# Hash attention and Fourier mixing on one core: masks and sums of the first head pairs on TensorE, a shorter float64 conversion, and another place for w2

## The chip, the cores and the metric

The kernel runs on one core of a Trainium2 chip. The metric is the time of one execution in microseconds (us) on the device; a median of several executions is quoted. One of the first three executions of the kernel before took 2249 us; the two others lie between 1431.8 and 1436.9 us (0.4%), so that one is left out of every comparison. Only fast runs are compared.

## The reference, cut to what matters

```python
# q, k, v: (4, 8, 768, 64) float32; proj: (64, 6)
q_bits = (q @ proj > 0)                        # 6 hash bits for each row, k alike
mask   = q_bucket[..., :, None] == k_bucket[..., None, :]
scores = where(mask, q @ k.T / 8, -1e9)
attn   = exp(scores - max);  attn = attn / (sum(attn) + 1e-9)
x      = (attn @ v), heads side by side        # (4, 768, 512)
mixed  = real(fft(fft(x, axis=1), axis=2))
u      = x + mixed
un     = (u - mean(u)) / sqrt(var(u) + 1e-6)
out    = u + maximum(un @ w_ch1, 0) @ w_ch2    # (512, 2048), (2048, 512): float64
```

The two weight matrices come as float64. The kernel reads them as pairs of 32-bit words and makes float32 of them: 16 chunks of 128 x 512 for w1, 16 for w2. That is the "conversion" of this text.

## The kernel before: the parts that matter

The attention works on 16 pairs of heads (four per batch), each in six steps of 128 keys. The mixing of batch b runs between the steps of the attention of batch b+1. During the four pairs of batch 0 (stage A from here on) there is no mixing yet, and w1 is converted beside them. During pair 4 and after it, the first mixing and the conversion of w2 run.

```python
def narrow(dst, src, name):                   # one chunk: nine DVE operations, one GpSimd add
    tag[0] ^= 1
    st = wt([P, 5 * WC], F32, "zF"[tag[0]], name, 1)   # staged in z's and in F's buffer by turns
    nc.gpsimd.dma_start(raw.bitcast(I64), src)
    ...
    nc.gpsimd.tensor_tensor(dst, val, rest, op=ALU.add)

def weigh(n, g, c, prep):                     # one step, one half of the queries
    ...                                       # two score matmuls (one per head) into PSUM
    nc.scalar.activation(pk[:, :, 0:HALF], ps[:, :, 0:HALF], AF.Exp, scale=SCALE)
    for h in range(2):                        # the mask: bucket equal, times exp
        nc.vector.scalar_tensor_tensor(
            pk[:, h, 0:HALF], qb[:, h, qs], kb[:, h, c : c + 1], pk[:, h, 0:HALF],
            op0=ALU.is_equal, op1=ALU.mult)
...                                           # in attention():
            nc.vector.tensor_tensor(accs[g], ..., new[g][:, :, 0:HALF], op=ALU.add)   # the sums
...                                           # in mix(): F is the mixing's own tile, and later
        hall = wt([P, NFC, HALF], F32, "F", f"h{b}", 1)   # the hidden layer takes its buffer
...
other = both(weights([(w2, moe_w_ch2)]), other)           # w2 beside the first mixing
```

(`z` and `F` are tiles of the mixing.) The small tiles in PSUM, the memory that matmuls write to (transposes, hash bits, means, closing sums, h), come from a pool that has two buffers while attention runs. Every engine's order of instructions is fixed when the kernel is compiled.

## Time and profile before

| what | kernel before | read from |
|---|---|---|
| median time | 1432.6 us | runs |
| stage A | 18 to 239 us | stretches |
| first matmul of h, the hidden layer | 306.9 us | timeline of PE |
| last chunk of w2 finished | 369.3 us | timeline of POOL |
| first transpose after h (un), batch 0 | 423.9 us | timeline of PE |

A line of the page gives the busy time of each engine over the whole span of 1430.6 us:

```profile
PE 1270.0 (89%) x4642; PEld 618.0 (43%) x4642; DVE 791.5 (55%) x1429; ACT 269.6 (19%) x433; POOL 142.9 (10%) x174
```

PE is at 89% over the span, so a change that takes nothing off PE can win at most the other 160 us. The shares alone mislead here: DVE's 55% is an average over a stage in which it is the bound and a long rest in which it isn't.

A measure is the length of a head pair. Each pair is closed by a few matmuls with output `sum` on PE, after its last step; the time from one such close to the next is one pair's length. For the kernel before, the timeline of PE gives 63.5, 60.3 and 33.1 us for the pairs 1, 2 and 3; the last of these leaves out a preparation (see the cautions below the table of the experiments). The last w1 chunk was finished at 201 us, in pair 3.

### The profile page before, as it was taken

The page shows a single profiled execution, that of the slowest core. Times are in us where ns is not written, and L with a number is a line of the kernel's source. Part 1 is how long each engine was busy: PE and PEld are TensorE (multiplying, and loading weights), DVE is VectorE, ACT ScalarE, POOL GpSimd, SP SyncE. Part 2 cuts the span into 40 slices and gives each one's busy share as a digit, 9 for nine tenths or more (in the row PEclk, how much of TensorE's full clock was granted, in tenths as well). Part 3 has the DMA queues.
Part 4 walks back from the last instruction along what each step waited for, and adds up shares of the span by engine and source line. Part 5 has one row for each costly group of instructions (what it writes and reads, how often), then busy time and mean ns, then how long its engine had stood idle before and what let it go on. Part 6 is the DMA issues. An engine that isn't in the chain of part 4 may idle for free.

```text
span 1430.6 us, 11986 instructions
## 1 busy us (share of the span) xinstructions
PE 1270.0 (89%) x4642; PEld 618.0 (43%) x4642; DVE 791.5 (55%) x1429; ACT 269.6 (19%) x433; POOL 142.9 (10%) x174
## 2 busy tenths in 40 slices
PE   6685677770799999989999999999999999899996
PEld 2221223440354444456544544374544444754552
DVE  6988989889743445485544463665434453511010
ACT  3122223200212121131212221222121211000000
POOL 1432220123100000000000000000000000001000
PEclk9787979995899999999999999999999999999999
DMA  6212121022101010010101010101010000000000
GB/s 162 75 47 78 40 67 48 30 80 94 37 0 41 15 34 8 7 41 8 27 8 41 8 34 14 42 0 34 0 41 15 1 8 8 8 0 12 11 8 17
DMA packets 82578, 44.65 MB, mean 31 GB/s; under 512 B 76496, under 2 KB 76624, under 8 KB 82384
## 3 DMA queue, kind: packets, MB, share of 16 engines
q1 hardware_dynamic: 75856, 20.72, 6.3%
q0 software_dynamic: 6656, 23.07, 5.1%
q8 instruction: 38, 0.62, 0.2%
q14 instruction: 28, 0.23, 0.1%
HBM read 37.49 MB, written 6.29 MB: 31 GB/s over the span
## 4 chain that ended last, share of the span: by engine, by line
PE 69%; DVE 8%; issue 2%; ACT 1%; POOL 1%; DMA 0%; ACTq 0%; DVEq 0%; POOLq 0%
PE o L909 23%; PE h L881 23%; PE sc L703 7%; PE oo L721 6%; PE cs L830 2%; PE B L856 2%; PE A L856 2%; DVE pk L711 1%; PE sum L738 1%; PE bits L664 1%; DVE acc L776 1%; DVE st L583 1%; PE un L897 1%; PE trk L647 1%; PE trq L647 1%
## 5 line engine op out<-in xcount | busy, mean ns | idle before, releaser
L881 PE MATMUL h<-x,w 128*128 128x384 f32 x1024 | 343.5, 492 | 52.8 <-ACT h L890 52.3
L909 PE MATMUL o<-w,h 128*128 128x512 f32 x768 | 343.5, 597 | 1.4 <-DVE h L888 1.4
L711 DVE SCALAR_TENSOR_TENSOR pk<-qb,kb,pk 128x384 f32<-128x384 bf16 x384 | 230.4, 638 | 176.8 <-ACT pk L709 176.8
L881 PEld LDWEIGHTS h<-x,w 128*128 128x128 f32 x1024 | 191.9, 191 | 203.0 <-ACT h L890 53.0
L709 ACT ACTIVATE pk<-sc 128x768 f32<-128x768 f32 x192 | 148.1, 810 | 392.8 <-PE sc L703 267.5
L909 PEld LDWEIGHTS o<-w,h 128*128 128x128 f32 x768 | 141.1, 190 | 179.5 <-issue 171.2
L721 PE MATMUL oo<-pk,vn 128*64 128x384 f32 (+1 forms) x768 | 185.5, 517 | 21.7 <-DVE pk L711 16.2
L703 PE MATMUL sc<-qt,kt 64*128 64x384 f32 x768 | 179.1, 532 | 9.8 <-ACT pk L709 8.9
L888 DVE TENSOR_SCALAR h<-h 128x384 f32<-128x384 f32 x64 | 35.6, 556 | 165.3 <-PE h L881 165.3
L776 DVE TENSOR_TENSOR acc<-acc,pk 128x768 f32<-128x768 f32 x128 | 120.6, 954 | 2.7
L703 PEld LDWEIGHTS sc<-qt,kt 64*128 64x128 f32 x768 | 73.3, 192 | 98.2 <-issue 51.1
L721 PEld LDWEIGHTS oo<-pk,vn 128*64 128x64 f32 x768 | 55.2, 138 | 127.4 <-issue 58.0
L601 POOL TENSOR_TENSOR w<-st 128x512 f32<-128x512 f32 x32 | 78.8, 2462 | 248.1 <-DVE st L598 248.1
L890 ACT ACTIVATE h<-h 128x384 f32<-128x384 f32 x64 | 31.4, 491 | 358.4 <-PE h L881 292.6
L915 DVE SCALAR_TENSOR_TENSOR u<-o,rs,u 128x512 f32<-128x512 f32 x24 | 18.0, 750 | 135.4 <-PE o L909 135.4
L905 POOL TENSOR_SCALAR rs<-mv 128x1 f32<-128x1 f32 x24 | 7.3, 304 | 557.4 <-DVE mv L903 557.2
L830 PE MATMUL cs<-ch,z 128*128 128x256 f32 x192 | 50.7, 414 | 9.0 <-DVE z L817 8.8
L800 POOL DMA_DIRECT2D out_dram<-u x32 | 19.6, 612 | 364.5 <-DVE u L915 257.0
L830 PEld LDWEIGHTS cs<-ch,z 128*128 128x128 f32 x192 | 37.2, 204 | 26.1 <-DVE z L817 11.8
L856 PE MATMUL A<-sq,F 128*128 128x193 f32 (+1 forms) x192 | 36.9, 329 | 1.2 <-DVE x L872 1.2
L856 PE MATMUL B<-sq,F 128*128 128x193 f32 (+1 forms) x192 | 36.6, 327 | 0.7 <-DVE F L837 0.5
L899 ACT COPY u<-un 128x512 f32<-128x512 f32 x24 | 14.0, 585 | 121.6 <-PE un L897 121.6
(81 smaller groups left out, 841.9 us busy)
## 6 DMA issues: line engine op xcount, KB each, us to landing
st<-in_moe_w_ch_dram POOLq DMA_DIRECT2D x32, 512.0 KB, 4.1
qn<-in_q_dram SPq DMA_DIRECT2D x32, 192.0 KB, 3.3
kn<-in_k_dram SPq DMA_DIRECT2D x32, 192.0 KB, 3.5
vn<-in_v_dram SPq DMA_DIRECT2D x32, 192.0 KB, 3.2
out_dram<-u POOLq DMA_DIRECT2D x16, 256.0 KB, 2.4
out_dram<-u POOLq DMA_DIRECT2D x16, 128.0 KB, 2.6
sq<-k_sq SPq DMA_DIRECT2D x1, 1155.0 KB, 6.0
ch<-k_ch SPq DMA_DIRECT2D x1, 512.0 KB, 3.6
```

Of the source, the lines that this page charges most:

```text
L601: nc.gpsimd.tensor_tensor(dst, val, rest, op=ALU.add)
L703: nc.tensor.matmul(ps[:, h, 0:HALF], kt[rows, c * P : (c + 1) * P], qt[rows, qs], start=True, stop=True,)
L709: nc.scalar.activation(pk[:, :, 0:HALF], ps[:, :, 0:HALF], AF.Exp, scale=SCALE)
L711: nc.vector.scalar_tensor_tensor(pk[:, h, 0:HALF], qb[:, h, qs], kb[:, h, c : c + 1], pk[:, h, 0:HALF], op0=ALU.is_equal, op1=ALU.mult,)
L721: nc.tensor.matmul(oo[h * D : (h + 1) * D, 0:w], nat["v", n][:, c, h, :], pk[:, h, 0:w], start=(c == 0), stop=(c == NT - 1),)
L776: nc.vector.tensor_tensor(accs[g], first[g][:, :, 0:HALF] if c == 1 else accs[g], new[g][:, :, 0:HALF], op=ALU.add,)
L830: nc.tensor.matmul(ps[:, pc:DM:2], z[:, cp, pc, par, t * P : (t + 1) * P], ch[:, cp, pc, :], start=(cp == 0), stop=(cp == 1),)
L856: nc.tensor.matmul(ps[:, cols], f, sq[:, t, k, cols], start=(t == 0), stop=(t == NT // 2 - 1),)
L881: nc.tensor.matmul(ps, w1[:, c, fc * P : (fc + 1) * P], x[:, c, g * HALF : (g + 1) * HALF], start=(c == 0), stop=(c == NDC - 1),)
L888: nc.vector.tensor_scalar(hr, ps, 0.0, None, op0=ALU.max)
L890: nc.scalar.activation(hr, ps, AF.Relu)
L909: nc.tensor.matmul(ps, hs[fc][:, j * P : (j + 1) * P], w2[:, fc, :], start=(fc == 0), stop=(fc == NFC - 1),)
```

## The change

The intent: DVE is full in stage A, so its mask multiplications and its sums go to TensorE for the pairs of batch 0 (masks up to pair 5); the conversion gets shorter on DVE, with its test of the exponent on ScalarE; w2 is staged in z's buffer alone and issued behind the first part of the mixing, so that no chunk of w2 lies in the buffer that the hidden layer waits for. The next pair is also prepared ahead (its transposes and hash bits made), between the steps of the current one. The matmul of the mask adds 0 to a score where all six bits agree and -2^33 or less where one differs, so that the exponential gives 0 there.

```diff
+            nc.gpsimd.tensor_scalar(qk[:, 0], qk[:, 0], BIG, None, op0=ALU.mult)   # +-BIG/2, +-1/2 bits
...
+        if kb is None:                        # mask as a matmul of bits, added to the scores in PSUM
+            for h, rows in enumerate(heads):
+                nc.tensor.matmul(ps[:, h, 0:HALF], qb[rows, 1, ks], qb[rows, 0, qs],
+                                 start=True, stop=False)
...
+            if sums is not None:              # batch 0: sums by four 32-column matmuls a step
+                for i in range(4):
+                    nc.tensor.matmul(sums[32 * i : 32 * i + 32, :], ones[:, 0:32],
+                                     pk[i // 2][:, i % 2, 0:HALF],
+                                     start=(c == 0), stop=(c == NT - 1))
...
+            if b == 0:
+                sums = pt([P, HALF], f"sums{n}")       # a small PSUM buffer, for the whole pair
+            else:
+                accs = [...]
...
+        nc.scalar.activation(mask, hi, AF.Abs)         # the test of the exponent, on ScalarE
+        nc.scalar.activation(mask, mask, AF.Abs, bias=mid[:, 0:1])
+        nc.scalar.activation(mi, mask, AF.Sign, bias=mid[:, 1:2])
...                                                    # then five DVE operations for nine
+            st = wt([P, 2, 3 * WC], F32, "z", f"st{wdr.shape[0]}", 1)     # two slots in z's buffer
...
+            ahead = prepare(n + 1) if n + 1 < NPAIR * B else iter(())
...
-            other = both(weights([(w2, moe_w_ch2)]), other)
+        other = after(NPAIR + NT, other, weights(w2, moe_w_ch2))
```

## The prediction

> **What bounds the kernel now.** I read the page's slices first, then the stretches, then the groups of the first stretch, then the waits of the gap. The slices show two different kernels in one span: for the first ten slices (358 us) TensorE (PE) is half to three quarters busy and its granted clock moves between 0.5 and 0.9, while VectorE (DVE) is near full; from slice 11 on PE is at 9 and the clock at full speed.
>
> ```profile
> PE   6685677770799999989999999999999999899996
> DVE  6988989889743445485544463665434453511010
> ACT  3122223200212121131212221222121211000000
> PEclk9787979995899999999999999999999999999999
> ```
>
> The stretches, cut where the trace has its stage borders (columns: length, busy us and instruction count of PE, weight load, DVE, ACT = ScalarE, POOL = GpSimd, then the clock):
>
> ```profile
> 18.00:239.00 221.00, 162.67 (x576) 54.50 (x577) 199.41 (x376) 54.84 (x84) 63.13 (x31) 0.84 0.24 61
> 239.00:307.00 68.00, 56.54 (x239) 34.90 (x240) 61.23 (x107) 12.85 (x18) 12.59 (x15) 0.92 0.11 35
> 307.00:365.00 58.00, 6.05 (x18) 2.98 (x18) 54.30 (x94) 0.15 (x1) 19.80 (x19) 0.59 0.30 102
> 365.00:409.00 44.00, 42.88 (x163) 22.03 (x164) 24.66 (x48) 11.09 (x20) 1.26 (x1) 0.96 0.08 18
> 409.00:1248.00 839.00, 825.62 (x3138) 410.94 (x3137) 425.94 (x756) 174.28 (x280) 34.12 (x72) 1.00 0.08 19
> ```
>
> From 18 to 239 us (stage A: head pairs 0 to 3 of batch 0, with w1 converted beside them) DVE is busy 199 of 221 us: it is the bound. From 239 to 307 (pair 4 and the mixing of batch 0) it still is. From 307 to 365 PE does nothing. After 365 PE never stops for long: it is the bound to the end. What DVE does in stage A, and what ended the gap:
>
> ```profile
> L711 DVE SCALAR_TENSOR_TENSOR pk<-qb,kb,pk 128x384 f32<-128x384 bf16 x96 | 62.2, 675 | 0.8 <-ACT pk L709 0.8
> L776 DVE TENSOR_TENSOR acc<-acc,pk 128x768 f32<-128x768 f32 x32 | 29.0, 946 | 0.0
> L592 DVE SCALAR_TENSOR_TENSOR st<-st 128x512 int32<-128x512 int32 x17 | 13.1, 771 | 0.0
> L583 DVE TENSOR_SCALAR st<-st 128x512 int32<-128x512 int32 x16 | 6.7, 417 | 0.0
> ```
>
> ```profile
> ACT h L890 <- POOL w L601: 65.7, 1, 65.7
> PEld h L881 <- ACT h L890: 53.0, 1, 53.0
> PE h L881 <- ACT h L890: 52.3, 1, 52.3
> ```
>
> The gap is a buffer wait: the tile that holds the hidden layer has the tag F, and the conversion of w2 stages every second chunk in that tag, so the first eviction of h waits for the last add (L601) of a w2 chunk in it. The timeline gives the pace there, one chunk per 5.53 us, DVE without a pause:
>
> ```profile
> 335.83 1.36 POOL L601 TENSOR_TENSOR w<-st 128x512 f32<-128x512 f32 x1 [3.31 <-DVE st L598]
> 337.49 0.55 POOL L572 DMA_DIRECT2D st<-in_moe_w_ch_dram  x1 [0.30 <-POOL w L601]
> 341.36 1.36 POOL L601 TENSOR_TENSOR w<-st 128x512 f32<-128x512 f32 x1 [3.31 <-DVE st L598]
> ```
>
> **What the Trainium skill says.** First, "ScalarE: Activation LUTs", What ACT_TABLE_LOAD costs: an ACTIVATE takes 186 ns and 0.833 ns an element, and about 93 ns more with a per-partition bias. The trace agrees: the exponential of 768 elements took 811 ns, the formula gives 826. Second, the same page, Table sets: cheap functions such as abs sit in every set, a change of set is a reload. The compiled change holds one table load, as before, so no reload is to be paid for Abs and Sign. Third, "TensorE: Matmul & The Clock Gate", Part 1: the array runs at half clock until it has been busy for one window of some 3.4 us and falls back after an idle one. The clock means 0.84 in stage A and 0.59 in the gap agree. Fourth, the same page, Part 3: matmuls in different 32-column strips run side by side. The four bit matmuls of 32 columns take 1.40 us at full clock here (833.90 to 835.30 us in the timeline), where four full ones would take 2.6 (the h rows: 24 instructions, 12 matmuls, in 7.94 us, so 0.66 us each).
>
> **The change, part by part.**
> DVE in stage A. Gone: 96 mask multiplications (62.2 us), all 40 acc additions (36 us), half the q and k evictions (5.4 us), the qb and kb copies (4.7 us). A chunk's conversion goes from nine DVE operations to five: 417 + 3 x 680 + 415 ns = 2.9 us where the rows of before add up to 5.0, so 16 chunks take 46 us where they took some 81. Added: 16 bit evictions of 0.55 us for 4 before (6.6 us). One reciprocal chain per pair for two saves about 8 us. What stays: 46 (conversion) + 9.9 (w1 minus its mean) + 11 (bits, with pair 5's) + 6.7 (reciprocals) + 4.8 (x) = 78 us, for 199. DVE is no bound any more.
>
> ScalarE in stage A. 48 exponentials x 0.81 = 39; evictions 20 x 0.415 + 10 x 0.478 = 13; squares 10; Abs, Abs with bias, Sign with bias per chunk 0.61 + 0.71 + 0.71 = 2.03 by the skill's formula, x 16 = 33; reciprocal evictions 4: 99 us for 55.
>
> PE per step (one block of 128 keys, 24 steps in stage A), full clock, from the rows of the steady part: scores 1.49, values 1.44; new masks about 0.4 (the four bf16 matmuls of 384 columns of qb took 0.43); sums of four 32-column matmuls 0.7 to 1.4, say 1.0; transposes and full-width bit matmuls (1.7 + 4 x 0.66) / 6 = 0.72; the two matmuls that spread the reciprocals 0.22; the means of w1 0.57. Sum 5.8 us. So PE alone would need 24 x 5.8 = 140 us.
>
> The conversion ring. Still two staging slots, and now each chunk goes through four engines in series. From the timeline: end of an add to the start of the next use of its slot 3.9 us (transfer and wake-up); three dependent ACT operations 2.1; four dependent DVE operations 2.6 (0.72 + 0.72 + 0.46 + 0.70); the add 1.35 with its wake-up. That is 10.1 us a slot, 5.05 us a chunk if nobody is in the way; among exponentials and evictions on the in-order ACT I take 12 us a slot, 6 a chunk. The compiled order puts the three ACT operations of all 16 w1 chunks ahead of the exponentials of step 10 or so of 24, thus the first steps go at the ring's pace.
>
> Sum to the end of stage A: first add at about 22 us as before (the start is the same load, transposes, bits); 7 more rounds x 12 = 84, the last chunk's Sign at about 101 us; 13.5 steps left at 5.8 plus some 0.7 for pair borders and single-buffered evictions (the sums hold one of the two small PSUM buffers throughout) = 88. Pair 4 starts at about 189 us where it started at 239: 50 us saved.
>
> Mixing and w2. The w2 slots lie in z's buffer, so the ring can start after the last cs matmul, which I put at pair 4's step 4: 189 + 28 = 217. Eight rounds of 12 us and a landing of 4 end it at about 317. In the compiled order the last w2 chunk stands on ACT beside h 12 and step 3 of pair 5; before reached that point at 409 us. So 92 us are saved there, not more, since PE alone would have been there 25 to 30 us sooner (h 12 x 2.65 + 2.5 steps x 4.1 + preparation, about 48 us after the first h at some 240). The gap of 52 us is gone, but part returns as ring waits between h matmuls.
>
> From there 1430.6 - 409 = 1022 us remain, the same work at the same full PE. Preparing the next pair ahead may take out the small waits at pair borders (0.7 us at pair 5, about 4 us at a batch border), 0 to 8 us in all. 317 + 1022 - 4 = 1335 us.
>
> **The rivals.** (1) The ring isn't felt: slots turn in 10 us, PE sets the pace. For it: the unloaded sum is 10.1, and DVE loses over half its load. Against it: both ACT and PE are in order, a wait for a transfer stands in front of an exponential. It would give 22 + 71 + 78 = 166 for stage A, the ring's end near 275, and 1295 us. (2) The chain gets longer than the ring: every exponential waits behind a conversion, every conversion behind an exponential that waits for PE at half clock; slots of 14 us, later steps of 7.5. For it: PE clock 0.84 in stage A already, one small PSUM buffer taken by the sums, 5.8 us then being an underestimate. It gives some 220 for pair 4 and 1385 us. (3) The expected gain is hidden because PE was the bound anyway. Against it: 52 us of plain PE idleness and 90% DVE in stage A; it would leave 1410 or so.
>
> **Range and chances.** The middle is 1335 us, between (1) and (2), nearer to (1) in mechanism but with the ring felt; 1300 to 1368 should hold it 8 times in 10. Even (2) is over 3% faster, so faster by over 2% has 0.97, within 2% 0.025, slower 0.005.
>
> **What would show it right or wrong.** DVE busy time in the stretch before pair 4 at about 80 us; ACT's idle time in its first 100 us ended by the w transfers; POOL adds of w1 every 6 us on average, the last near 105; pair 4's scores starting at 180 to 200 us; no PE gap above some 8 us after 20 us, but short PE waits on ACT during w2; the last w2 add at 310 to 325; 1015 to 1022 us from h 12 to the end. If adds come every 7 us or more, rival 2 holds; if PE is dense before the last w2 add, rival 1. The prediction fails most easily if the clock stays low in stage A or the adds on POOL stretch (they average 3.2 us before 270 us in the profile of before, 1.4 in the median).

## The result, and the profile after

The changed kernel takes 1350.48 us (median of 4, 1346.92 to 1354.56). The ratio to the kernel before is 0.942, with a 95% interval of 0.9375 to 0.9466. Ratios in this text are the mean time of one kernel's fast runs over that of the other's fast runs of the same rounds, so they are not quite the ratio of the quoted medians. A second set of five runs gave 0.9401 (x_after2 below).

The slices of the changed kernel, each 33.6 us long:

```profile
PE   5889999989999999999999999999999998999995
...
DVE  2655225886344626744444626754344635310110
...
PEclk9979999999999999999999999999999999999998
```

The hole in PE's row is gone, DVE's row has no 9 left, and from the fourth slice to the last but one PE is at 8 or 9 with the clock up. The stretches of the changed kernel, cut at its own stage borders (columns as in the prediction: length, then busy time and count of PE, weight load, DVE, ACT, POOL, then the clock):

```profile
18.00:199.00 181.00, 162.00 (x795) 60.80 (x798) 81.19 (x141) 86.69 (x142) 42.05 (x38) 0.94 0.28 75
118.00:199.00 81.00, 79.45 (x408) 29.98 (x408) 19.68 (x37) 29.43 (x48) 5.71 (x5) 1.00 0.13 30
232.00:328.00 96.00, 83.95 (x346) 47.06 (x344) 76.68 (x132) 47.53 (x74) 28.81 (x30) 0.96 0.31 99
```

Stage A is now 181 us (18 to 199), and DVE is busy for 81 of them where it was for 199 of 221. But look at the second line: in the second half of stage A PE is busy for 79.45 of 81 us at a clock of 1.00. DVE has 61 idle us there. The bound has moved to PE.

How long a pair takes with next to nothing left to convert can be read between the first exponentials of two pairs on ACT: such a stretch holds six steps and one preparation in both kernels. Pair 3 of the kernel before (columns as above):

```profile
200.32:240.38 40.06, 32.29 (x142) 12.23 (x140) 39.06 (x77) 13.09 (x21) 1.26 (x1) 0.94 0.13 30
```

And pair 2 of the changed kernel:

```profile
118.17:158.48 40.31, 39.46 (x204) 14.99 (x202) 7.91 (x15) 14.65 (x24) 2.91 (x3) 1.00 0.13 30
```

The pair takes 40.1 us before and 40.3 after. What has changed is the engine that is full: DVE before (39.06 us), PE after (39.46 us). So on its own a pair has not become faster; the change gains where the conversion used to hold DVE.

### The profile page after: what moved, and what is told of

It reads as the page before. It is cut to its first block, busy times and chain, and to the rows that moved or that the text cites. A ratio compares the mean times of both kernels' runs of the same rounds, so it can differ in the third digit from the quotient of the medians.

```text
span 1345.0 us, 12355 instructions
## 1 busy us (share of the span) xinstructions
PE 1275.1 (95%) x4902; PEld 631.4 (47%) x4902; DVE 610.6 (45%) x1081; ACT 337.1 (25%) x549; POOL 127.9 (10%) x192
## 4 chain that ended last, share of the span: by engine, by line
PE 78%; issue 7%; DVE 6%; POOL 3%; DMA 2%; ACT 2%; POOLq 0%; SPq 0%; ACTq 0%; DVEq 0%
PE o L987 25%; PE h L959 24%; PE sc L752 9%; PE oo L772 8%; PE cs L908 3%; DMA st<-in_moe_w_ch_dram 2%; POOL w L613 2%; DVE pk L761 2%; PE B L934 2%; PE A L934 2%; PE sum L808 1%; PE sums L827 1%; DVE acc L853 1%; PE un L975 1%; ACT pk L758 1%
## 5 line engine op out<-in xcount | busy, mean ns | idle before, releaser
L959 PE MATMUL h<-x,w 128*128 128x384 f32 x1024 | 344.4, 494 | 9.6 <-ACT qt L516 4.1
L761 DVE SCALAR_TENSOR_TENSOR pk<-qb,kb,pk 128x384 f32<-128x384 bf16 x240 | 137.7, 613 | 178.7 <-ACT pk L758 178.7
L752 PE MATMUL sc<-qt,kt 64*128 64x384 f32 x768 | 204.1, 515 | 2.5 <-ACT pk L758 2.5
L772 PE MATMUL oo<-pk,vn 128*64 128x384 f32 (+1 forms) x768 | 154.6, 505 | 0.8 <-DVE x L813 0.8
L752 PEld LDWEIGHTS sc<-qt,kt 64*128 64x128 f32 x768 | 83.3, 188 | 80.4 <-issue 59.0
L853 DVE TENSOR_TENSOR acc<-acc,pk 128x768 f32<-128x768 f32 x96 | 93.0, 972 | 15.0 <-ACT pk L758 13.2
L772 PEld LDWEIGHTS oo<-pk,vn 128*64 128x64 f32 x768 | 47.9, 137 | 94.5 <-issue 82.4
L613 POOL TENSOR_TENSOR w<-w,st 128x512 f32<-128x512 f32 x32 | 43.0, 1342 | 120.2 <-DVE st L610 109.9
L908 PE MATMUL cs<-ch,z 128*128 128x256 f32 x192 | 46.2, 389 | 4.3 <-DVE x L813 2.5
L592 ACT ACTIVATE st<-st 128x512 f32<-128x512 int32 x32 | 21.9, 684 | 60.4 <-DMA st<-in_moe_w_ch_dram 60.4
```

What stands on the lines that cost most here:

```text
L613: nc.gpsimd.tensor_tensor(dst, dst, rest, op=ALU.add)
L752: nc.tensor.matmul(ps[:, h, 0:HALF], kt[rows, ks], qt[rows, qs], start=kb is not None, stop=True,)
L761: nc.vector.scalar_tensor_tensor(pk[:, h, 0:HALF], qb[:, h, qs], kb[:, h, c : c + 1], pk[:, h, 0:HALF], op0=ALU.is_equal, op1=ALU.mult,)
L772: nc.tensor.matmul(oos[g][h * D : (h + 1) * D, 0:w], nat["v", n][:, c, h, :], pk[g][:, h, 0:w], start=(c == 0), stop=(c == NT - 1),)
L853: nc.vector.tensor_tensor(accs[g], first[g][:, :, 0:HALF] if c == 1 else accs[g], new[g][:, :, 0:HALF], op=ALU.add,)
L908: nc.tensor.matmul(ps[:, pc:DM:2], z[:, cp, pc, par, t * P : (t + 1) * P], ch[:, cp, pc, :], start=(cp == 0), stop=(cp == 1),)
```

## The experiments

Every experiment is an edit of the changed kernel. The first four ran on one chip, the next four on the same chip, the last four on another chip; the first and the last had their own runs of the kernel before, the second used those of the first and one more. All results are correct except that of x_noconv. The pair lengths are from the timeline of PE.

| run | us, median | ratio | 95% interval | pair 0 closes at | pairs 1, 2, 3 take | first un |
|---|---|---|---|---|---|---|
| before | 1432.6 | 1 | | 70.6 | 63.5, 60.3, 33.1 | 423.9 |
| changed kernel | 1350.5 | 0.942 | 0.9375 to 0.9466 | 77.9 | 45.6, 40.3, 38.3 | 336.9 |
| x_dvetest | 1353.5 | 0.9438 | 0.9423 to 0.9454 | 80.6 | 45.9, 40.3, 38.3 | 344.4 |
| x_raw3 | 1347.8 | 0.9401 | 0.9384 to 0.9417 | 82.8 | 41.8, 40.8, 38.3 | 334.6 |
| x_nolite | 1349.1 | 0.9422 | 0.9402 to 0.9443 | 63.8 | 46.7, 52.5, 40.6 | 335.6 |
| x_w1nine | 1348.9 | 0.9409 | 0.9392 to 0.9426 | 78.4 | 44.3, 40.5, 38.3 | 338.9 |
| x_noconv (wrong result) | 1313.9 | 0.9168 | 0.9146 to 0.9189 | 67.4 | 40.2, 40.5, 38.3 | 304.6 |
| x_sumsdve | 1323.7 | 0.9236 | 0.922 to 0.9251 | 62.1 | 44.8, 40.9, 28.0 | 313.1 |
| x_noahead | 1350.1 | 0.942 | 0.9405 to 0.9436 | 73.0 | 52.9, 34.7, 32.1 | 340.0 |
| x_onlyw2 | 1377.9 | 0.9616 | 0.96 to 0.9632 | 71.3 | 59.1, 58.5, 33.1 | 361.6 |
| x_hold | 1335.0 | 0.9304 | 0.9277 to 0.9331 | 63.7 | 43.3, 42.8, 32.7 | 320.7 |
| x_w2order | 1386.1 | 0.9657 | 0.9641 to 0.9673 | 78.7 | 49.9, 44.0, 38.3 | 375.2 |
| x_sums_raw3 | 1320.5 | 0.9202 | 0.9184 to 0.9219 | 66.9 | 43.3, 34.5, 28.0 | 306.4 |
| x_after2 (changed kernel) | 1350.0 | 0.9401 | 0.9383 to 0.942 | 76.5 | 46.8, 40.4, 38.3 | 337.3 |

Two cautions about the closes. With the sums on PE a close waits for the reciprocal on DVE and comes after the next pair's first scores: the last value matmuls of pair 0 start at 66.64 us in the changed kernel and its close at 77.91, where x_sumsdve has 60.79 and 62.13. And without preparing ahead (before, x_noahead, x_onlyw2) the closes of the pairs 0 to 2 come after the next pair's preparation, that of pair 3 before it, so the number for pair 3 lacks a preparation there. Where this matters, the text goes by the start of a pair's first exponential on ACT ("starts").

### x_dvetest: the exponent test back on DVE

```diff
-        nc.scalar.activation(mask, hi, AF.Abs)
-        nc.scalar.activation(mask, mask, AF.Abs, bias=mid[:, 0:1])
-        nc.scalar.activation(mi, mask, AF.Sign, bias=mid[:, 1:2])
+        nc.vector.tensor_scalar(mi, hi, 2**31 - 1, None, op0=ALU.bitwise_and)
+        nc.vector.tensor_scalar(mi, mi, float(897 << 20), -1.0, op0=ALU.is_ge, op1=ALU.mult)
```

> The changed kernel with one part undone: the exponent test of a conversion chunk goes back from three ScalarE operations (2.1 us in series) to two on VectorE (0.84 us). Theory ring: stage A and the w2 stage go at the pace of two staging slots, 13 us a round for w1 and 12 for w2 in the trace of the changed kernel; the round gets 1.2 us or more shorter and no exponential stands behind a transfer any more, so 7 rounds of w1 and 8 of w2 give 18 to 30 us: 1318 to 1330 us. Rival PE: PE and the small PSUM buffers set the pace, the ring is hidden: 1340 to 1352 us. Rival DVE: VectorE is still short in the w2 stage (77 of 96 us busy), 32 x 0.84 us more on it cost time: 1355 to 1370 us.

Measured: 1353.5 us, 3 us more by the medians, with intervals that overlap (0.9423 to 0.9454 against 0.9375 to 0.9466). What ScalarE took over in this part of the change is worth some 3 us, if anything.

### x_raw3: three staging slots

```diff
-            st = wt([P, 2, 3 * WC], F32, "z", ...)       # two slots of raw words and mask
+            st = wt([P, 3, 2 * WC], F32, "z", ...)       # three slots of raw words
-                    narrow(dst, src, s[:, 0 : 2 * WC].bitcast(I32), s[:, 2 * WC :])
+                    mask = wt([P, WC], F32, "u", ..., 2) # the mask in a buffer that is idle then
+                    narrow(dst, src, st[:, n % 3].bitcast(I32), mask)
```

> The changed kernel with three raw staging slots in the same bytes for two (the mask goes to a buffer that is idle then), nothing else changed. Theory ring: a round of 12 to 13 us now serves three chunks, 4.2 us a chunk where it was 6 to 6.5; stage A becomes PE's (pair 4's scores at about 180 us for 199.7) and the last w2 add comes by about 295 us for 327.5; 1300 to 1318 us. Rival PE: no change, 1340 to 1352 us. Rival ScalarE: the three operations on ScalarE themselves, not the slots, hold up the exponentials: between, 1325 to 1340 us.

This is the test of the prediction's pacing: if the ring of two slots sets the pace of the first steps, a third slot shortens them. Measured: the last w1 chunk was finished at 98.5 us where the changed kernel had 117.2, so the ring did turn faster, and the attention did not: pair 0 closes 5 us later, pair 1 takes 4 us less, the pairs 2 and 3 the same within 0.5 us, and the time is 1347.8 us, with an interval (0.9384 to 0.9417) that lies inside that of the changed kernel. What PE waits for has changed instead. The waits of PE in x_raw3 between 20 and 120 us (total us, times, longest):

```profile
PE sum L803 <- DVE rb L790: 5.8, 1, 5.8
PE bitsq L692 <- DVE qkb L693: 4.5, 1, 4.5
```

In the changed kernel the same two rows are 2.9 and 2.5. The conversions that come earlier stand on DVE, which works in the compiled order, among the operations of a reciprocal and in front of a bit eviction (at the end of pair 0, from the copy of `vs` to the last transpose of the reciprocal, six conversion operations stand between, 76.04 to 82.22 us, where the changed kernel has four, 72.51 to 77.27). So the number of slots isn't the bound.

### x_nolite: masks and sums back on DVE

```diff
-    LITE = 6
+    LITE = 0
-            if b == 0:
+            if b < 0:                                    # no sums on PE
-                elif b > 0:
+                elif b >= 0:                             # DVE sums in every batch
```

> The changed kernel with the first part undone: all masks and sums on VectorE again, the new conversion and the new place of w2 kept. Theory: VectorE's load before pair 4 goes from 80 us to about 185, so pair 4's scores start at 210 to 222 us for 199.7, and the w2 stage gets 31 us more VectorE work: 1368 to 1390 us. Rival: the new conversion alone already freed VectorE enough, the masks on TensorE only moved work: 1340 to 1355 us.

Measured: 1349.1 us, the same as with them on PE. DVE is full again (91.14 of 98 us between 20 and 118 us, 59.73 in the changed kernel), and in sum it costs nothing: pair 1 starts 9 us earlier than in the changed kernel (59.6 and 69.0 us), pair 3 at the same time (158.8 and 158.5). The first part of the change as a whole is worth zero beside the other parts; x_sumsdve below shows that this zero is a gain and a loss.

### x_w1nine: nine DVE operations for w1

The edit gives w1 the conversion of before, staged in the F buffer, which is idle in stage A; w2 keeps the short one.

```diff
+            if wsb is w1:
+                st = wt([P, 2, 5 * WC], F32, "F", "st_w1", 1)
...
+                    if wsb is w1:
+                        narrow9(dst, src, s)             # the nine operations of before
```

> The changed kernel with the nine VectorE operations of before for w1 alone (staged in two slots of the buffer that the mixing uses later), w2 as changed. Theory ring: with the masks gone VectorE has room for 16 x 2.1 us more, and ScalarE loses 33 us; the round stays near 12 us, pair 4's scores come at 190 to 203 us and the time is 1335 to 1352 us, so the shorter conversion is worth next to nothing in stage A. Rival: the saved VectorE operations are a real part of the gain there: 1360 to 1375 us.

Measured: 1348.9 us, no difference, though DVE is at 90.19 of 98 us between 20 and 118 us. With the masks and sums on PE, the shorter conversion of w1 is worth nothing either.

### x_noconv: hardly any conversion, with a wrong result on purpose

```diff
-        nc.scalar.activation(mask, hi, AF.Abs)
...                                                       # all ACT and DVE operations go
-        nc.gpsimd.tensor_tensor(dst, dst, rest, op=ALU.add)
+        nc.gpsimd.tensor_tensor(dst, hi.bitcast(F32), hi.bitcast(F32), op=ALU.add)
```

> Wrong result on purpose: the changed kernel with the conversion cut to its transfer and one GpSimd add a chunk; the eight ScalarE and VectorE operations are gone for both weights, so a round of the two slots falls to about 5.3 us (3.9 + 1.35). Three slots changed nothing (1347.8 us), so the slot count is not what holds stage A. Theory blocking: a conversion costs PE by standing in front of other work on in-order engines (in the run with three slots PE waited 5.8 and 4.5 us for VectorE, which had conversions ahead); without it pairs 0 and 1 take about the 40.4 us of pairs 2 and 3 instead of 49, and the w2 stage loses its 12 us of PE idleness: 1312 to 1326 us. Rival PE: the conversion is hidden behind PE's own work as it is: 1338 to 1350 us.

Measured: 1313.9 us (relative error 285.6). Both conversions together still cost 36 us in the changed kernel. More telling are the closes of the pairs 2 and 3 (timeline of PE in x_noconv):

```profile
148.16 1.56 PE L781 MATMUL sum<-rb,sel 128*128 128x384 f32 x4 [0.71 <-DVE rb L768]
...
186.48 1.56 PE L781 MATMUL sum<-rb,sel 128*128 128x384 f32 x4 [0.71 <-DVE rb L768]
```

Pair 3 takes the same 38.3 us, pair 2 takes 40.5 (40.3 in the changed kernel), and even pair 1 still takes 40.2 with no conversion at all. So a pair of the changed kernel takes 38 to 40 us because of PE's own work. By the closes, the conversion of w1 costs the changed kernel 77.9 - 67.4 = 10.5 us in pair 0 and 45.6 - 40.2 = 5.4 in pair 1, nothing in the pairs 2 and 3; that of w2 costs 77.7 - 66.9 = 10.8 us between the first h matmul and the first un (259.19 to 336.88 in the changed kernel, 237.65 to 304.56 here), and 57.0 - 51.2 = 5.8 before that, from the close of pair 3 to the first h matmul.

### x_sumsdve: masks on PE, sums on DVE

If PE is the bound, the next question is which of its new jobs is worth the place.

```diff
-            if b == 0:
+            if b < 0:                                    # no sums on PE
-                elif b > 0:
+                else:                                    # DVE sums in every batch
```

> Masks stay on TensorE, the denominators of batch 0 go back to VectorE additions. Theory PE: pairs 2 and 3 show PE dense (78.5 of 80 us) at 6.7 us a step, of which the sums take 0.79 and the spreading 0.25; so without them stage A is some 15 to 20 us shorter, VectorE (20 of 80 us busy there) has room for the 44 us: 1325 to 1336 us. Rival conversion: the first 100 us hang on the conversion, VectorE gets 22 us more in them and is in front of PE: 1345 to 1360 us.

Measured: 1323.7 us, 27 us faster than the changed kernel, with a correct result and DVE work put back. The closes of the pairs 2 and 3 in x_sumsdve (timeline of PE):

```profile
147.83 1.46 PE L808 MATMUL sum<-acc,ones 128*64 128x384 f32 x8
...
175.82 1.46 PE L808 MATMUL sum<-acc,ones 128*64 128x384 f32 x8
```

Pair 3 takes 28.0 us for 38.3 (163.83 to 202.16 in the changed kernel). With x_nolite as the third corner: masks and sums on DVE 1349.1, masks on PE and sums on DVE 1323.7, both on PE 1350.5 us. The masks on PE are worth 25 us; the sums on PE cost 27. In the traces x_sumsdve starts pair 1 7.0 us earlier than the changed kernel, pair 2 6.7, pair 3 12.7 and pair 4 22.5: the gain lies in the pairs 0, 2 and 3, and pair 1, beside the conversion (which ends at 130.6 us here), gains nothing.

Why so much, when the sums of a step took only 0.79 us? One step of the changed kernel, with half of the next pair's bit matmuls in it, from one start of the sums to the next (timeline of PE):

```profile
143.67 0.85 PE L827 MATMUL sums<-pk,ones 128*32 128x384 f32 x8
144.46 0.91 PE L692 MATMUL bitsq<-qt,pjw 128*128 128x384 f32 x2
145.30 0.34 PE L747 MATMUL sc<-qkb 64*128 64x384 bf16 x2
145.47 0.81 PE L752 MATMUL sc<-qt,kt 64*128 64x384 f32 x2
146.21 0.91 PE L692 MATMUL bitsq<-qt,pjw 128*128 128x384 f32 x2
147.05 0.59 PE L752 MATMUL sc<-qt,kt 64*128 64x384 f32 x1
...
148.70 1.51 PE L772 MATMUL oo<-pk,vn 128*64 128x385 f32 x8
150.14 0.53 PE L827 MATMUL sums<-pk,ones 128*32 128x384 f32 x4
```

And the same kind of step in x_sumsdve:

```profile
136.96 0.34 PE L747 MATMUL sc<-qkb 64*128 64x384 bf16 x2
137.13 0.81 PE L752 MATMUL sc<-qt,kt 64*128 64x384 f32 x4
137.78 0.33 PE L747 MATMUL sc<-qkb 64*128 64x384 bf16 x2
137.94 0.81 PE L752 MATMUL sc<-qt,kt 64*128 64x384 f32 x4
138.68 1.51 PE L772 MATMUL oo<-pk,vn 128*64 128x385 f32 x8
140.12 1.56 PE L692 MATMUL bitsk<-kt,pjw 128*128 128x384 f32 x4
141.61 0.34 PE L747 MATMUL sc<-qkb 64*128 64x384 bf16 x2
```

A float32 matmul is two records here, so "sc<-qt,kt x4" is the two heads of one block and "x2" one head alone. The two heads use 64 rows of the array each, and run side by side: 137.13 to 137.78, 0.65 us for both. In the changed kernel the first head's matmul alone takes 145.47 to 146.21, 0.74 us, then a bit matmul stands between, then the second head starts. The scores and masks of a step take 1.72 us in x_sumsdve (136.96 to 138.68) and 0.91 + 1.65 = 2.56 us in the changed kernel (145.30 to 146.21 and 147.05 to 148.70); the two bit matmuls 1.49 in one go and 1.68 one by one. The step as a whole takes 6.47 us (143.67 to 150.14) and 4.65 (136.96 to 141.61): 0.79 us of the difference are the sums, 0.84 the split scores, 0.19 the single bit matmuls. A step with transposes pays as much: 5.73 us (176.54 to 182.27) for 3.97 (159.91 to 163.88). Counted in the traces over the 48 score blocks of stage A, 20 are split by another matmul in the changed kernel and none in x_sumsdve.

The Trainium skill bears on this: "TensorEngine Tiling (Array Packing)", Key Properties, says that changing the tiling mode, as opposed to the tile, drains the array. A bit matmul uses all 128 rows, a score matmul 64, so the split also adds changes of mode. The trace shows the cost of both together, not that of the drain alone.

### x_noahead: no preparing ahead

```diff
-            ahead = prepare(n + 1) if n + 1 < NPAIR * B else iter(())
+            if n > 0:
+                for _ in prepare(n):
+                    pass
-                if c > 0:
-                    next(ahead, None)
```

> The part of the change that its title does not name undone: the next pair is prepared at its own start again instead of step by step during the pair before. Theory: the preparation chain (transposes, evictions, bits, masks) is exposed at each border: 4 borders in stage A of 5 to 8 us and 10 later ones of 0.5 to 1 us: 1365 to 1385 us. Rival: PE has enough other work to hide it, as from 365 us on in the kernel before: 1345 to 1355 us.

Measured: 1350.1 us, no difference in the end, but not the same inside. By their starts, the pairs 0 and 1 take 53.2 and 51.6 us with the transposes and bits at the pair's start (47.8 and 49.2 with preparing ahead), pair 2 takes 37.9 (40.3) and pair 3 42.2 (42.3); pair 4 starts 4.5 us later, and the first un comes 3.1 us later. That the medians agree all the same is within the spread: the profiled run is the slowest of its four here and the fastest of its four in the changed kernel. The trace shows one thing more. Although the sums hold their PSUM buffer, none of the 48 score blocks of stage A is split when nothing is prepared between the steps, and a step takes 3.95 us (its value matmuls start at 173.97, 177.91, 181.86 and 185.81 us).

### x_onlyw2: only the part of w2

The masks and sums are on DVE (as in x_nolite), w1 has its nine operations (as in x_w1nine), nothing is prepared ahead (as in x_noahead); w2 keeps its new place and the short conversion.

```diff
+    LITE = 0; no sums on PE; narrow9 for w1; prepare(n) at the pair's start
     other = after(NPAIR + NT, other, weights(w2, moe_w_ch2))     # kept
```

> Only w2's part of the change: its new place and its five VectorE operations; masks and sums on VectorE, nine operations for w1 and preparation at the pair's start as before. Theory: the gap of 52 us goes, stage A stays as long as before (first cs matmul at 245 us where the changed kernel has 209), so 1380 to 1400 us. Rival: the place of w2 is all that counted, 1345 to 1360 us.

Measured: 1377.9 us, ratio 0.9616. Of the 83 us that the change saves, w2's part alone brings 55. The other 29 us come with the shorter w1 conversion and preparing ahead (x_nolite, 1349.1), or else with masks and sums on PE and preparing ahead (x_w1nine, 1348.9), and with all of them no more (1350.5). This does not mean that DVE had room to spare after the first relief: in x_nolite it is still busy for 91.14 of 98 us, and with the short conversion in place the masks on PE bring 25 us (x_nolite against x_sumsdve). It is the sums on PE that take them back.

### x_hold: a small PSUM buffer held, with hardly any work

```diff
 # on top of x_sumsdve, in batch 0
+                hold = pt([P, HALF], f"hold{n}")
...
+            if hold is not None and c in (0, NT - 1):
+                nc.tensor.matmul(hold[0:D, 0:2], ones, pk[0][:, 0, 0:2],
+                                 start=(c == 0), stop=(c == NT - 1))
...                                           # at the end one column of it is copied out by DVE
```

> The kernel with the masks on TensorE and the sums on VectorE (1323.7 us), plus one of the two small PSUM buffers held through each pair of batch 0, by one two-column matmul at the pair's first block and one at its last. That is next to no TensorE work. Theory A: most of what the sums on TensorE cost (about 27 us) comes from the buffer that they hold, which lets transposes and bit matmuls go only one at a time between the score matmuls; then 1338 to 1350 us, and as many score pairs split by another matmul as in the changed kernel (28 of 82). Theory B: the cost is the matmuls of the sums themselves (0.8 us a step, 24 steps, 19 us[...]); then 1322 to 1330 us. Between the two: both have a share, read off in proportion.

Measured: 1335.0 us, between the two theories, so both have a share: by the ratios the held buffer costs 0.9304 - 0.9236 = 0.0068, about 10 us, and the sums' own matmuls 0.9401 - 0.9304 = 0.0097, about 14 us (the first difference is between two chips). In the traces pair 4 starts at 178.2, 185.1 and 200.8 us in x_sumsdve, here and in the changed kernel, which gives 7 and 16. Of the 48 score blocks of stage A 18 are split; the count in the expectation is another one. The trace of x_hold shows a step with two bit matmuls (timeline of PE):

```profile
168.56 1.51 PE L772 MATMUL oo<-pk,vn 128*64 128x385 f32 x8
170.00 0.91 PE L692 MATMUL bitsq<-qt,pjw 128*128 128x384 f32 x2
...
171.75 0.91 PE L692 MATMUL bitsq<-qt,pjw 128*128 128x384 f32 x2
...
174.24 1.19 PE L772 MATMUL oo<-pk,vn 128*64 128x385 f32 x6
```

From one start of the value matmuls to the next it takes 174.24 - 168.56 = 5.68 us: 1.03 us above x_sumsdve's 4.65 and 0.79 below the changed kernel's 6.47. So the split is the doing of the held buffer, where something is prepared between the steps (x_noahead, with the buffer held and nothing prepared there, has no split): with one small PSUM buffer left, the second bit matmul can't start before the first is evicted, and the compiled order puts half of a score block in between.

### x_w2order: the place of w2 undone

```diff
-            st = wt([P, 2, 3 * WC], F32, "z", ...)
+                    s = wt([P, 3 * WC], F32, "Fz"[n % 2], ..., 1)       # F's and z's buffer by turns
-            other = after(NPAIR + NT, other, weights(w2, moe_w_ch2))
+            other = both(weights(w2, moe_w_ch2), other)
```

> The changed kernel with only the place of w2 put back: its chunks are staged in z's and the hidden layer's buffers by turns, and started before the first mixing is issued. Theory: the gap before the first eviction of the hidden layer comes back, shorter than the 52 us of before since a chunk now takes less of VectorE, some 20 to 40 us; 1370 to 1390 us. Rival: the shorter conversion alone takes the gap away, since VectorE needs 2.9 us a chunk and not 5; then 1345 to 1358 us.

Measured: 1386.1 us, 36 us more than the changed kernel. The first line of PE's waits in x_w2order between 200 and 400 us:

```profile
PE h L959 <- ACT h L968: 34.4, 1, 34.4
```

Not all of the 36 us is the gap: pair 4 starts 9 us later than in x_after2 (209.5 and 200.6 us). In stage A three chunks of w2 are now converted (their additions come at 125, 136 and 148 us), and the edit changes w1's staging tiles too; the two are not told apart. The gap is back, at 34.4 us for the 52.3 of before. So the placement takes away a gap that the shorter conversion alone leaves at two thirds. The run also measures a term of the prediction: in the gap nothing but conversion runs, and the additions into one slot follow at 280.22, 290.55 and 300.98 us, 10.4 us a round where the prediction put 10.1 for the unloaded ring (its four terms add up to 9.95).

### x_sums_raw3 and x_after2: the best version, beside the changed kernel

The first is x_sumsdve with x_raw3's three slots; the second is the changed kernel again.

```diff
 # x_sums_raw3: x_sumsdve and
+            st = wt([P, 3, 2 * WC], F32, "z", ...)
```

> Masks on TensorE, sums on VectorE, and three staging slots for the raw 64-bit words (the mask in a buffer that is idle then). With TensorE's steps back at 5 us or less, the conversion may be what paces the first steps again. Theory A: the third slot now pays, 1308 to 1319 us. Theory B: it stays without effect, as in the changed kernel, since the in-order queues pay for a conversion that is nearer as much as for one that is late: 1320 to 1327 us.

> The changed kernel again, on the chip of the three others, for comparison with them: 1346 to 1355 us.

Measured: 1320.5 us for x_sums_raw3 (0.9202), 1350.0 for the changed kernel (0.9401) on the same chip: a correct version that beats both kernels, by 29.5 and 115 us. The third slot seems to bring some 3 us now (pair 2 takes 34.5 us for 40.9 in x_sumsdve), but the intervals (0.9184 to 0.9219 and 0.922 to 0.9251) all but touch, so this is left unsettled: the median lies at the lower edge of theory B's range, 1.5 us from theory A's.

## Why the prediction was right, and where it was wrong

The verdict and the range hold: 1350.5 us within 1300 to 1368, faster by 5.8%. It is 15.5 us above the predicted 1335. In the profiled run (1345.0 us) the prediction is 10 us short, and all of it is lost before pair 4: pair 4's scores start at 199.66 us for 189, and from there to the end are 1145.3 us for 1146.

**Right.** The two bounds named: DVE in stage A, and the buffer wait of the hidden layer (x_w2order brings it back, x_onlyw2 shows 55 us for w2's part). DVE's busy time before pair 4, 81.2 us for 78 (from 18 us on); ACT's, 86.7 for 99 (94.9 with the first 18 us). One table load and none more: the Trainium skill, "ScalarE: Activation LUTs", Table sets, let expect this for Abs, and the prediction had it for both functions from the compiled change. The formula of the same page, What ACT_TABLE_LOAD costs, gave 0.71 us for the Abs and Sign with bias, and the trace has 0.72. In the w2 stage the round of the ring, (327.49 - 243.29) / 7 = 12.03 us for 12, and no PE wait above 2.8 us. The last w2 addition came at 327.5 us for 317, late by what was lost before; from it to the end 1017.5 us for 1018.

**The step that failed: "thus the first steps go at the ring's pace".** The ring did turn at about the pace predicted, (117.17 - 25.85) / 7 = 13.05 us a round for 12, and it ended near step 11, as the prediction had read from the compiled order. But it did not set the pace. x_raw3 finished w1 almost 19 us sooner and gained no step; x_noconv, without a conversion to wait for, ran its pairs 1 to 3 at 40.2, 40.5 and 38.3 us. PE itself needs that long. The conversion cost 16 us in all, in pair 0 and pair 1. Rival (1) of the prediction had the mechanism, that PE sets the pace, but with 5 to 6 us a step; its sum for stage A is also wrong, 22 + 71 + 78 being 171 and not 166, so that it would have said some 1300 us and not 1295.

**The term that was mis-sized: "Sum 5.8 us" a step of PE.** The rows were each close: the sums 0.79 us where it says 1.0, scores and masks side by side 1.72 where 1.49 and 0.4 add up to 1.89. Missing is what the parts do to each other. A pair takes 38.3 to 40.3 us, 6.4 to 6.7 a step: a step with bit matmuls pays 1.03 us, one with transposes about as much, because the sums hold a small PSUM buffer and the score blocks are split (x_hold). The prediction saw the held buffer, and put 0.7 us a step for it and the borders together, so its 6.5 us for the later steps fits; that it fits is luck in part, since the allowance was argued as waits, and PE shows hardly any in the second half of stage A (79.45 of 81 us busy).

That is also why two faults all but cancelled. Ten and a half steps at the ring's supposed pace are 79 us, 7.5 us a step; PE's own pace is 6.5. The wrong mechanism and the right one are only 10 us apart over the first half.

**What the prediction did not ask.** It counted what left DVE and not whether the same work is cheaper where it went. With w1 converted, a pair of the changed kernel takes as long as one of the kernel before (40.3 and 40.1 us between starts), and without the sums on PE pair 3 is 10 us shorter (28.0 for 38.3 between closes). The masks on PE gained 25 us, the sums gave 27 back.

**The smaller terms.** "Preparing the next pair ahead", entered as 4 us, brought nothing: from the first un to the end the kernel before takes 1430.6 - 423.9 = 1006.7 us and the changed one 1345.0 - 336.9 = 1008.1; x_noahead has the same median. The multiplication of the bits by BIG on GpSimd was not in the prediction at all; it takes 2.17 us a pair, and PE waits for it at most 1.4 us at a time in the runs. Two of the signs that the prediction set itself missed: the last w1 addition came at 117.2 us and not near 105, the last of w2 at 327.5 and not by 325. And its first reading is loose: of the first ten slices, said to be half to three quarters busy on PE, the third shows an 8 and the tenth, in the gap, a 0.

**What stays open.** In pair 0 and pair 1 the conversion costs 16 us, but neither a third slot, nor the test on DVE, nor nine operations for w1 move the time by more than about 3 us. Which of the in-order queues (ACT or DVE) holds the steps there was not isolated. Nor was the drain of a change of tiling mode separated from the loss of side-by-side running.

## What to carry to other kernels

Before moving work off a full engine, work out what the receiving engine does alone once the full one is relieved; if it becomes the bound, what is moved costs time there. Test the moved parts one by one: here a gain of 25 us and a loss of 27 stood behind a part that seemed to be worth nothing. An accumulator that stays in PSUM over a loop takes a buffer from everything that shares its pool (7 to 10 us here): look in the compiled order for what then comes between matmuls that run side by side on parts of the array. And test a pacing argument by the thing that paces: a third slot took one run here, and showed that the ring was not the bound. Before comparing two lengths, see that the same work lies in both: the closes of pair 3 seemed to say that a pair had become 5 us longer.

## What the Trainium skill lacked or had wrong

- "TensorEngine Tiling (Array Packing)", Key Properties, has the drain at a change of tiling mode but no cost and no warning about order. Here a full-array matmul between the two 64-row halves of a score block, and the changes of mode with it, made a step 5.68 us long where it was 4.65.
- "TensorE: Matmul & The Clock Gate", Part 3, has a measured speedup for three column tiles, and for four only together with row tiles. Four 32-column float32 matmuls of 384 columns took 0.79 us here, where one full-size one in a row of such took 0.66: about 3.3 times the rate.
- "ScalarE: Activation LUTs", What ACT_TABLE_LOAD costs: the formula fits the operations with a bias (0.72 us measured, 0.71 by formula), but Abs on every second int32 word of 128 x 512 took 0.69 us where it gives 0.61. The page doesn't speak of such inputs.
- "GPSIMD Engine Reference", section 3.1, has figures for float32 additions and a best case of 1.8 cycles an element. A bf16 multiplication by a constant on 128 x 768 took 2.17 us here (POOL spans are rough in these profiles), 2.8 ns an element, where an estimate from that best case gives 1.15 us and one from the 1.03 cycles that the page has for short bodies 0.66.
- No page tells what an accumulating tile costs the other users of its pool of PSUM buffers; "Perfetto Trace Analysis" only names too few buffers as a possible cause of repeated gaps. Here one of two buffers held for a pair cost 7 to 10 us over four pairs.
